# Weight conversion and attention in one scheduling region: earlier stores of finished weight blocks and a first operand cast in three pieces

## The chip, the cores and the metric

The kernel runs on one core of one Trainium2 chip. The metric is the device time of one execution in microseconds (us), from the median of several runs. The core's engines are named as the profile names them: PE (TensorE, matrix products; PEld is its weight load), DVE (VectorE), ACT (ScalarE), POOL (GpSimd) and SP (SyncE), whose queue issues nearly all transfers of this kernel. Each engine works through its own list of instructions in the order in which the list stands.

## The reference

Sigmoid attention for 8 batches of 12 heads (448 positions, 64 wide), whose output, 3584 rows of 768, goes through a gated feed-forward layer.

```python
scores = scale * np.matmul(q, k.transpose(0, 1, 3, 2)) - np.log(S)
attn = 1.0 / (1.0 + np.exp(-scores))
x = np.matmul(attn, v)            # then (batch, position) x (head, width)
gate = 1.0 / (1.0 + np.exp(-(x @ w_gate)))
return (gate * (x @ w_val)) @ w_out
```

The three weights are 64-bit floats: `w_gate` and `w_val` 768 x 1536, `w_out` 1536 x 768.

## The kernel before

**Attention.** A loop of 168 beats (24 times four heads, 7 beats each). In each beat PE forms scores for one tile (line 220), ACT takes their sigmoid (line 223), and PE multiplies the sigmoid of two beats earlier with the values (line 239), into PSUM tiles that exist once each. When such a tile is complete, twice in seven beats, ACT copies one half of it to SBUF (line 263) and DVE adds the other half (`finish_adds`, line 309). Only then may PE begin the next product in that tile, which is four beats later.

**Weights.** `Units.steps` (lines 118 to 159) turns the 64-bit weights into 32-bit floats and forms seven blocks for each unit of work: three of them (`a11`, `a12`, `a22`) are quarters of the tile `wf`, which DVE fills, and four are sums and differences in `wsum`, which POOL fills. There are two `wf` buffers, two `wsum` buffers and three buffers `wr` for the raw weights, which SP loads (line 115). A unit is a generator of steps: for each of its two halves three DVE instructions (lines 124 to 126), then line 128, then line 130; POOL's four sums belong to the last step. The first four units are used in place (13 steps each); the blocks of the other fourteen go to DRAM by seven transfers (line 158). These are put into a list of delayed work, `after(4, store)`, when the generator is called again after the unit's last step, so in the first step of the next unit; they are issued four calls of `tick` later. A tick is one beat in attention, one group of nine products in the feed-forward part.

Steps 1 to 64 are called in the attention loop, one in about 2.4 beats (steps 53 to 58 are the fifth unit, 59 to 64 the sixth). The other 73 are called in the feed-forward loop. A table `turns` gives each operand of that loop a share, and after every group of products steps are called until their part of the 73 has caught up with the part of the shares that is done. In the kernel before, the first operand of all has the share 6 in each of its four groups; of 576 shares in all, its 24 stand for steps 65 to 68.

**Feed-forward.** 300 groups of nine products (line 401) for the gate and value weights, with 25 operands in each of three passes and four groups for each operand; then 50 operands for the output weight. An operand is loaded (`load_x`, line 174, two buffers `src`), its high part is cast by ACT (`high_x`, line 177) into the tile `op` and its low part is formed by DVE (`low_x`, line 180). Both are made for the first operand near the end of the attention loop: the load at the 160th beat, the cast of all 1536 columns at the 164th, the low part at the 165th.

**Order.** Attention stands in one `tc.manual_schedule()` block, the feed-forward part in a second. The program gives the order in which the instructions are written; the scheduler makes each engine's list from it.

Of the kernel before, what the change touches and what calls it, by code (L numbers as in the profile page):

```python
# [14 lines left out]
PSUM = bass.MemoryType.PSUM  # L15
# [24 lines left out]
def sigmoid_attention_glu_kernel(ctx: ExitStack, tc: tile.TileContext, qk, v, wg, wv, wo, out):  # L40
    nc = tc.nc
# [34 lines left out]
    def after(n, fn, store=True):  # L76
        later.append((clock[0] + n, fn, store))

    def tick(flush=False):
        clock[0] += 1  # L80
        due = [e for e in later if e[0] <= clock[0] or flush and e[2]]
        later[:] = [e for e in later if e not in due]
        for _, fn, _ in due:
            fn()
# [6 lines left out]
    def op_tile():  # L91
        return keep.tile([P, 2, 3, F], F32R, tag="op", name="op", bufs=3)
# [4 lines left out]
    def block(tag, n, shape, dtype):  # L97
        return keep.tile(shape, dtype, tag=tag, name=tag, bufs=n)

    class Units:  # L100
# [17 lines left out]
        def steps(self):  # L118
            for s, q, w, j in self.todo:
                f = block("wf", 2, [P, 2, DM], U32)  # L120
                for r in range(2):
                    raw = self.loaded.pop(0)
                    a = f[:, r]
                    nc.vector.tensor_scalar(out=a, in0=raw[:, :, 1], scalar1=0x7FFFFFFF, scalar2=None, op0=ALU.bitwise_and)  # L124
                    nc.vector.tensor_scalar(out=a.bitcast(F32), in0=a.bitcast(F32), scalar1=F64_ZERO, scalar2=None, op0=ALU.max)  # L125
                    nc.vector.tensor_scalar(out=a, in0=a, scalar1=3, scalar2=0x3FFFFFF8, op0=ALU.logical_shift_left, op1=ALU.bitwise_and)
                    yield
                    nc.vector.scalar_tensor_tensor(out=a, in0=raw[:, :, 1], scalar=0xC0000000, in1=a, op0=ALU.bitwise_and, op1=ALU.bitwise_or)  # L128
                    yield
                    nc.vector.scalar_tensor_tensor(out=a, in0=raw[:, :, 0], scalar=29, in1=a, op0=ALU.logical_shift_right, op1=ALU.bitwise_or)  # L130
                    after(2, self.load)
                    if r == 0:
                        yield
                ff = f.bitcast(F32)
                if s < NPASS:
                    a11, a12, a21, a22 = ff[:, 0, :HW], ff[:, 0, HW:], ff[:, 1, :HW], ff[:, 1, HW:]
                else:
                    a11, a21, a12, a22 = ff[:, 0, :HW], ff[:, 0, HW:], ff[:, 1, :HW], ff[:, 1, HW:]
                ss = block("wsum", 2, [P, 4, HW], F32)
                s1, s2, s3, s4 = (ss[:, n] for n in range(4))  # L140
                sub = lambda o, a, b: nc.gpsimd.tensor_tensor(out=o, in0=a, in1=b, op=ALU.subtract)
                nc.gpsimd.tensor_tensor(out=s1, in0=a21, in1=a22, op=ALU.add)  # L142
                sub(s2, s1, a11)
                sub(s3, a11, a21)
                sub(s4, a12, s2)
                blocks = [a11, a12, s2, s3, a22, s1, s4]
                yield
                if s == 0:
                    for i in range(NP):
                        nc.gpsimd.tensor_copy(W[i][:, q, 0], blocks[i])  # L150
                        nc.vector.tensor_tensor(out=W[i][:, q, 1], in0=blocks[i], in1=W[i][:, q, 0].bitcast(F32), op=ALU.subtract)
                        yield
                else:
                    to = [w_src[s][i][:, q] if s < NPASS else o_src[i][:, q] for i in range(NP)]

                    def store(to=to, blocks=blocks):
                        for t, b in zip(to, blocks):
                            nc.sync.dma_start(out=t, in_=b)  # L158
                    after(4, store)

    units = Units()
    weights = units.steps()
# [5 lines left out]
    x_loaded, ops = {}, {}  # L168
# [7 lines left out]
    def high(op, src):  # L176
        nc.scalar.copy(op[:, 0], src)  # L177
# [4 lines left out]
    def high_x(n):  # L182
        if n < len(x_order):
            ops[n] = op_tile()
            high(ops[n], x_loaded[n])
# [4 lines left out]
            load_x(n + 2)  # L190

    halves = (slice(0, HP), slice(HP, P))
    with tc.manual_schedule(), tc.tile_pool(name="att", bufs=2) as att, tc.tile_pool(name="sc", bufs=2, space=PSUM) as scp, \
            tc.tile_pool(name="av", bufs=1, space=PSUM) as avp:
        loads, avs, pending, adds = {}, {}, [], []

        def load_qk(m):
            if m < B * NQ:
                loads[m] = [att.tile([P, 2, 2 * S], F32, tag="qk", name="qk")]
                if m > 0:  # L200
                    nc.sync.dma_start(out=loads[m][0], in_=qk[m // NQ, m % NQ])
# [10 lines left out]
        def scores(m, g):  # L212
            qkt = loads[m][0]

            sc = second_pair() if (m, g) == (0, LAG) else scp.tile([P, 2, 512], F32, tag="sc", name="sc")
            for h in range(2):
                for u in range(2):
                    p = u if g == 3 else g // 4
                    k0 = S + (3 * P if g == 3 else g % 4 * P + u * HP)
                    nc.tensor.matmul(sc[halves[u], h, :S], lhsT=qkt[halves[h], p, k0:k0 + HP], rhs=qkt[halves[h], p, :S],  # L220
                                     start=True, stop=True)
            a = att.tile([P, 2, S], F32, tag="a", name="a", bufs=3)
            nc.scalar.activation(a, sc[:, :, :S], AF.Sigmoid, bias=bias, scale=scale)  # L223
            return a

        def values(m, g, a):
            vt = loads[m][1]
            for u in range(2):
                p = u if g == 3 else g // 4
                key = (2 * m + p, u)  # L230
                start = g == (3 + (u == 0) if p else 0)
                if start and p == 0:
                    avs[key] = avp.tile([P, 512], F32, tag=f"av0{u}", name="av")
                elif start and u == 1:
                    pair = second_pair()
                    avs.update({(2 * m + p, w): pair[:, w] for w in range(2)})
                last = (3 if u == 0 else 2) if p == 0 else 6
                for h in range(2):
                    nc.tensor.matmul(avs[key][halves[h], :S], lhsT=vt[halves[u], g, h], rhs=a[halves[u], h],  # L239
                                     start=start, stop=g == last)  # L240
            if g == 3:
                finish(2 * m)
            if g == 6:
                finish(2 * m + 1)
# [21 lines left out]
        def sub(o, a, b):  # L266
            nc.gpsimd.tensor_tensor(out=o, in0=a, in1=b, op=ALU.subtract)
# [79 lines left out]
        sc = scp.tile([P, 2, 512], F32, tag="sc", name="sc")  # L347
# [5 lines left out]
        beats, beat, done = B * NQ * 7, 0, 0  # L353
        for m in range(B * NQ):
            for g in range(7):
                pending.append((m, g, scores(m, g)))
                if len(pending) > LAG:
                    values(*pending.pop(0))
                if g == 0:
                    load_qk(m + 1)  # L360
                if g == LAG:
                    load_v(m + 1)
                if m == 0 and g <= LAG:
                    units.load()
                tick()
                beat += 1
                while done < N_FIRST and done * (beats - 12) < beat * N_FIRST:
                    next(weights)
                    done += 1
                finish_adds()  # L370
                if beat > 24 and sum(map(len, later_parts)):
                    next(w for w in later_parts if w).pop(0)()
                if beat == beats - 8:
                    load_x(0)
                    load_x(1)
                if beat == beats - 4:
                    high_x(0)
                if beat == beats - 3:
                    low_x(0)
        while pending:  # L380
# [4 lines left out]
        low_x(1)  # L385
        tick(flush=True)

    with tc.manual_schedule(), tc.tile_pool(name="mm", bufs=8, space=PSUM, reuse_waits="tile") as mm:

        def bank():  # L390
            return mm.tile([P, F], F32, tag="mm", name="acc")
# [56 lines left out]
        with tc.tile_pool(name="ff", bufs=1, reuse_waits="tile") as ff:  # L448
# [3 lines left out]
            def store_h(p, i, j, h):  # L452
# [4 lines left out]

            turns = {(s, p, r): (6, 5, 3, 3, 1, 1, 1)[r] if SETS[p] is PAIR else (6, 5)[r % 2]
                     for s in range(NPASS) for p in range(NSET - (1 if s < NPASS - 1 else 2)) for r in range(len(SETS[p]))
                     if s == 0 or p > 0 or r > 1}  # L460
            done, groups, all_groups = 0, 0, sum(turns.values()) * NQUAD
            for s in range(NPASS):
                for p in range(NSET):
# [4 lines left out]
                    for r, (i, _) in enumerate(SETS[p]):  # L468
                        for q in range(NQUAD):
                            d, t, jl = st[q], q % 2, q // 2  # L470
# [30 lines left out]
                            elif i in (2, 3):  # L501
                                k = "u2" if i == 2 else "u3"
                                d[k] = unit(k, 4)
                                add(d[k], acc, d["s1"])
                            else:
                                k, to = {4: ("s1", 1), 5: ("u3", 6), 6: ("u2", None)}[i]
# [160 lines left out]
```

## Time and profile before

| | |
|---|---|
| median of 3 runs | 1190.94 us (1190.78 to 1191.88) |
| profiled execution | 1191.03 us, of which the span from its first to its last instruction is 1189.2 us |
| PE busy | 1178.9 us, 99% of the span |
| DVE, ACT, POOL busy | 59%, 41%, 25% of the span |
| DMA engines | 65.3% busy for SP's queue |
| mean clock granted to PE | 0.997 of full speed |

A matrix product's row in the trace is longer than the distance to the next one, since products are pipelined and their ends are modelled. Where PE's pace matters, the number of products in a stretch of time says more than the busy share. Idle time in square brackets stands before an instruction, with what ended it.

### The profile page before, as it was taken

The numbers are of one execution on the slowest core, as the hardware profiler recorded it, in microseconds if no ns is written. First come the engines' busy times: TensorE is split into PE (matmuls) and PEld (weight loads), VectorE is DVE, ScalarE is ACT, GpSimd is POOL, SyncE is SP. The second block draws the span as 40 slices with busy tenths as digits, with TensorE's granted clock in tenths as the row PEclk, the third lists the DMA queues.
The fourth block names the chain that finished last, engine by engine and source line by source line (L and its number), as shares of the span: only waits on it lengthen the run. The fifth ranks groups of instructions, "written<-read, shape, count | busy, mean of one in ns | idle before, by whom it ended". The sixth has DMA issues, their size and how long they took to land.

```text
span 1189.2 us, 17012 instructions
## 1 busy us (share of the span) xinstructions
PE 1178.9 (99%) x6754; PEld 860.8 (72%) x6754; DVE 698.3 (59%) x725; ACT 488.6 (41%) x514; POOL 297.5 (25%) x232
## 2 busy tenths in 40 slices
PE   9999999899999999999999999999999999999998
PEld 3333333348888888888888888888888888888887
DVE  3334334436798848889875888747676542244343
ACT  6777777663323234432232532323445212422320
POOL 1335225143182332344322344404020000000000
PEclk9999999989999999999999999999999999999999
DMA  8588867776588675758857666755876553445431
GB/s 302 166 244 287 268 231 240 259 266 227 208 311 289 237 272 198 245 189 291 313 195 283 227 227 220 256 184 191 292 246 249 177 203 133 156 153 186 170 115 71
DMA packets 105376, 266.95 MB, mean 224 GB/s; under 512 B 19920, under 2 KB 54736, under 8 KB 105296
## 3 DMA queue, kind: packets, MB, share of 16 engines
q1 hardware_dynamic: 105152, 265.73, 65.3%
q8 instruction: 53, 0.87, 0.3%
q14 instruction: 27, 0.22, 0.1%
q10 hardware_dynamic: 144, 0.13, 0.0%
HBM read 178.91 MB, written 86.90 MB: 224 GB/s over the span
## 4 chain that ended last, share of the span: by engine, by line
PE 97%; DMA 1%; DVE 1%; SPq 0%; ACT 0%; issue 0%; DVEq 0%; ACTq 0%
PE acc L401 77%; PE sc L220 10%; PE av L239 10%; DMA wr<-wg 1%; DMA ws<-wf 0%; DMA qk<-qk 0%; SPq L158 0%; DVE wf L130 0%; DVE op L309 0%; DVE wf L124 0%; ACT a L223 0%; DVE wf L128 0%; SPq L270 0%; PE av L220 0%; DVE wf L125 0%
## 5 line engine op out<-in xcount | busy, mean ns | idle before, releaser
L401 PE MATMUL acc<-op,w 128*128 128x512 f32 x3600 | 828.3, 389 | 0.0
L401 PEld LDWEIGHTS acc<-op,w 128*128 128x128 f32 x3600 | 675.8, 188 | 140.8 <-issue 0.7
L180 DVE TENSOR_TENSOR op<-src,op 128x1536 fp32r<-128x1536 f32 x125 | 236.2, 1900 | 106.0 <-ACT op L177 84.3
L177 ACT CAST op<-src 128x1536 fp32r<-128x1536 f32 x125 | 184.6, 1479 | 196.9 <-PE acc L401 162.9
L223 ACT ACTIVATE a<-sc,bias 128x896 f32<-128x896 f32 x167 | 168.1, 1007 | 73.8 <-PE sc L220 69.1
L239 PE MATMUL av<-a,v 64*64 64x448 f32 x1344 | 168.0, 541 | 5.6 <-DVE op L309 5.6
L220 PE MATMUL sc<-qk 64*64 64x448 f32 x1336 | 167.9, 545 | 0.1
L239 PEld LDWEIGHTS av<-a,v 64*64 64x64 f32 x1344 | 53.7, 134 | 83.1 <-issue 74.2
L220 PEld LDWEIGHTS sc<-qk 64*64 64x64 f32 x1336 | 53.0, 135 | 80.2 <-issue 67.7
L408 DVE TENSOR_TENSOR u<-acc,s 128x512 f32<-128x512 f32 x90 | 61.7, 688 | 78.8 <-PE acc L401 78.7
L408 DVE TENSOR_TENSOR u<-acc,u 128x512 f32<-128x512 f32 (+1 forms) x91 | 61.7, 682 | 64.4 <-PE acc L401 63.8
L520 POOL TENSOR_TENSOR t<-u,v 128x512 f32<-128x512 f32 x17 | 26.6, 1566 | 283.6 <-DVE u L411 233.3
L142 POOL TENSOR_TENSOR wsum<-wf 128x384 f32<-128x384 f32 x18 | 19.9, 1106 | 201.2 <-DVE wf L130 201.2
L513 ACT ACTIVATE u<-u 128x512 f32<-128x512 f32 x36 | 22.7, 632 | 97.5 <-DVE u L408 97.5
L408 DVE TENSOR_TENSOR s<-acc,s 128x512 f32<-128x512 f32 x45 | 31.0, 689 | 34.2 <-PE acc L401 34.2
L513 ACT ACTIVATE s<-s 128x512 f32<-128x512 f32 x18 | 11.4, 632 | 96.1 <-DVE s L408 96.1
L401 PE MATMUL acc<-op,wr 128*128 128x512 f32 x198 | 50.2, 389 | 0.0
L309 DVE TENSOR_TENSOR op<-av,op 128x448 f32<-128x448 f32 x24 | 15.0, 623 | 52.6 <-ACT op L263 52.6
L309 DVE TENSOR_TENSOR x<-av,x 128x448 f32<-128x448 f32 x24 | 15.0, 624 | 49.5 <-ACT x L263 49.5
L124 DVE TENSOR_SCALAR wf<-wr 128x768 uint32<-128x768 uint32 x36 | 26.9, 748 | 28.4 <-DMA wr<-wg 17.2
L401 PEld LDWEIGHTS acc<-op,wr 128*128 128x128 f32 x198 | 37.2, 188 | 7.7
L436 DVE TENSOR_TENSOR w<-w 128x1536 fp32r<-128x1536 f32 x21 | 41.1, 1959 | 0.0
(61 smaller groups left out, 723.2 us busy)
## 6 DMA issues: line engine op xcount, KB each, us to landing
src<-xs SPq DMA_DIRECT2D x75, 768.0 KB, 5.1
src<-hs SPq DMA_DIRECT2D x50, 768.0 KB, 5.2
qk<-qk SPq DMA_DIRECT2D x23, 896.0 KB, 5.0
hs<-t SPq DMA_DIRECT2D x78, 256.0 KB, 6.0
w<-ws SPq DMA_DIRECT2D x14, 768.0 KB, 7.1
v<-vv SPq DMA_DIRECT2D x23, 448.0 KB, 4.5
wr<-wg SPq DMA_DIRECT2D x12, 768.0 KB, 6.9
wr<-wv SPq DMA_DIRECT2D x12, 768.0 KB, 6.7
```

Source lines behind the costliest of these rows:

```text
L124: nc.vector.tensor_scalar(out=a, in0=raw[:, :, 1], scalar1=0x7FFFFFFF, scalar2=None, op0=ALU.bitwise_and)
L177: nc.scalar.copy(op[:, 0], src)
L180: nc.vector.tensor_tensor(out=op[:, 1], in0=src, in1=op[:, 0].bitcast(F32), op=ALU.subtract)
L220: nc.tensor.matmul(sc[halves[u], h, :S], lhsT=qkt[halves[h], p, k0:k0 + HP], rhs=qkt[halves[h], p, :S], start=True, stop=True)
L223: nc.scalar.activation(a, sc[:, :, :S], AF.Sigmoid, bias=bias, scale=scale)
L239: nc.tensor.matmul(avs[key][halves[h], :S], lhsT=vt[halves[u], g, h], rhs=a[halves[u], h], start=start, stop=g == last)
L309: nc.vector.tensor_tensor(out=x, in0=other, in1=x, op=ALU.add)
L401: nc.tensor.matmul(acc, lhsT=a, rhs=b, start=first and n == 0 and half != 1, stop=n == len(terms) - 1 and half != 0, skip_group_check=not ...
L408: nc.vector.tensor_tensor(out=o, in0=a, in1=b, op=ALU.add)
L436: nc.vector.tensor_tensor(out=w[:, :, 1], in0=w[:, :, 1].bitcast(F32), in1=w[:, :, 0].bitcast(F32), op=ALU.subtract)
L513: nc.scalar.activation(d[k], d[k], AF.Sigmoid)
L520: nc.gpsimd.tensor_tensor(out=o, in0=a, in1=b, op=ALU.subtract)
```

## The change

There are four edits. The store of a unit's blocks is split: the three blocks in `wf` are issued after one tick, the four in `wsum` still after four. Both parts of the kernel stand in one `manual_schedule` block, which is entered once for the whole function. The first operand's load moves from the 160th to the 159th beat, its `op` tile is taken there too, and its cast is made as three casts of 512 columns in beats 162, 163 and 164. The first operand's four groups have no share in `turns` any more, which leaves 552 shares; step 65 is then called in the first group of the second operand.

```diff
-                    def store(to=to, blocks=blocks):
-                        for t, b in zip(to, blocks):
-                            nc.sync.dma_start(out=t, in_=b)
-                    after(4, store)
+                    def store(which, to=to, blocks=blocks):
+                        for i in which:
+                            nc.sync.dma_start(out=to[i], in_=blocks[i])
+                    after(1, lambda store=store: store((0, 1, 4)))
+                    after(4, lambda store=store: store((2, 3, 5, 6)))
...
-    with tc.manual_schedule(), tc.tile_pool(name="att", bufs=2) as att, tc.tile_pool(name="sc", bufs=2, space=PSUM) as scp, \
+    ctx.enter_context(tc.manual_schedule())
+    with tc.tile_pool(name="att", bufs=2) as att, tc.tile_pool(name="sc", bufs=2, space=PSUM) as scp, \
             tc.tile_pool(name="av", bufs=1, space=PSUM) as avp:
...
-                if beat == beats - 8:
+                if beat == beats - 9:
                     load_x(0)
                     load_x(1)
-                if beat == beats - 4:
-                    high_x(0)
+                    ops[0] = op_tile()
+                if beats - 7 < beat < beats - 3:
+                    k = beat - beats + 6
+                    nc.scalar.copy(ops[0][:, 0, k], x_loaded[0][:, k])
...
-    with tc.manual_schedule(), tc.tile_pool(name="mm", bufs=8, space=PSUM, reuse_waits="tile") as mm:
+    with tc.tile_pool(name="mm", bufs=8, space=PSUM, reuse_waits="tile") as mm:
...
-                     if s == 0 or p > 0 or r > 1}
+                     if (p > 0 or r > 1 if s > 0 else p + r > 0)}
```

## Rows read from the trace of the kernel before

**Rows 1.** Longest piece of the chain of waits: start us, us, what.

```profile
267.35 918.24 PE acc L401 x4050
```

**Rows 2.** Busy time by stretch: length, each engine's busy us, PE clock, DMA.

```profile
20.00:228.20 208.20, 208.20 (x2220) 79.21 (x2214) 79.45 (x115) 156.21 (x179) 75.25 (x90) 1.00 0.75 245
228.20:267.27 39.07, 33.42 (x316) 14.26 (x310) 13.17 (x19) 22.64 (x26) 14.15 (x12) 0.91 0.74 256
245.38:267.27 21.89, 21.89 (x232) 10.23 (x224) 4.62 (x5) 16.95 (x19) 10.85 (x10) 1.00 0.87 302
239.50:245.38 5.88, 5.87 (x32) 2.04 (x36) 3.25 (x5) 1.01 (x1) 3.31 (x3) 0.51 0.35 100
```

**Rows 3.** Timeline of PE, two instructions: start us, us, engine, line [idle before].

```profile
230.00 0.59 PE L239 MATMUL av<-a,v 64*64 64x448 f32 x2 [0.88 <-DVE op L309]
...
239.51 1.01 PE L239 MATMUL av<-a,v 64*64 64x448 f32 x2 [4.76 <-DVE op L309]
```

**Rows 4.** Timeline of DVE from 218 us, and its first weight step after 267 us.

```profile
218.49 0.95 DVE L128 SCALAR_TENSOR_TENSOR wf<-wr,wf 128x768 uint32<-128x768 uint32 x1
225.67 0.56 DVE L124 TENSOR_SCALAR wf<-wr 128x768 uint32<-128x768 uint32 x1 [6.23 <-DMA ws<-wf]
...
229.33 0.62 DVE L309 TENSOR_TENSOR op<-av,op 128x448 f32<-128x448 f32 x1
229.86 0.95 DVE L130 SCALAR_TENSOR_TENSOR wf<-wr,wf 128x768 uint32<-128x768 uint32 x1
...
238.36 0.56 DVE L124 TENSOR_SCALAR wf<-wr 128x768 uint32<-128x768 uint32 x1 [5.88 <-DMA wr<-wg]
...
280.51 0.95 DVE L128 SCALAR_TENSOR_TENSOR wf<-wr,wf 128x768 uint32<-128x768 uint32 x1
```

**Rows 5.** Timeline of SP's queue in the same stretch.

```profile
230.84 0.32 SPq L158 DMA_DIRECT2D ws<-wf  x1
...
232.18 0.42 SPq L115 DMA_DIRECT2D wr<-wg  x1
```

**Rows 6.** Waits of SP's queue: who waited for whom: us, times, longest us.

```profile
SPq L158 <- DVE wf L130: 7.4, 1, 7.4
```

**Rows 7.** Timelines of ACT and PE around the first operand's cast.

```profile
258.59 0.52 ACT L263 COPY x<-av 128x448 f32<-128x448 f32 x1
259.19 1.01 ACT L223 ACTIVATE a<-sc,bias 128x896 f32<-128x896 f32 x1
260.10 1.47 ACT L177 CAST op<-src 128x1536 fp32r<-128x1536 f32 x1
261.46 1.90 ACT L223 ACTIVATE a<-sc,bias 128x896 f32<-128x896 f32 x2
...
261.55 0.54 PE L220 MATMUL sc<-qk 64*64 64x448 f32 x2
...
262.52 1.07 PE L220 MATMUL sc<-qk 64*64 64x448 f32 x8
```

**Rows 8.** ACT's casts by shape: count | busy us, mean ns | idle before.

```profile
L433 ACT CAST w<-w 128x1536 fp32r<-128x1536 f32 x21 | 30.9, 1473 | 0.0
...
L433 ACT CAST wr<-wr 128x768 fp32r<-128x768 f32 x3 | 2.5, 825 | 0.0
```

**Rows 9.** Operand loads, us to landing: whole execution, then those issued from 250.8 us.

```profile
src<-xs SPq DMA_DIRECT2D x75, 768.0 KB, 5.1
...
src<-xs SPq DMA_DIRECT2D x2, 768.0 KB, 8.2
```

**Rows 10.** Early feed-forward part: two stretches, then two DVE instructions.

```profile
275.50:324.50 49.00, 49.00 (x218) 40.59 (x217) 36.55 (x43) 15.31 (x16) 7.17 (x6) 1.00 0.65 223
324.50:349.00 24.50, 24.50 (x109) 20.28 (x108) 24.19 (x20) 5.53 (x5) 20.34 (x11) 1.00 0.83 272
...
269.35 2.60 DVE L180 TENSOR_TENSOR op<-src,op 128x1536 fp32r<-128x1536 f32 x1 [0.76 <-ACT op L177]
...
333.45 1.64 DVE L124 TENSOR_SCALAR wf<-wr 128x768 uint32<-128x768 uint32 x1
```

## The prediction

> **What bounds the kernel now.** I read the chain of waits first. Its last piece is 4050 products of the feed-forward part, one after another for 918.24 us [rows 1]: 226.7 ns each without a gap, so nothing done there for DVE, ACT or the queues can shorten those 918 us. They begin at 267.35 us. What can still move is therefore the attention part before them, and I compared its pace by stretch. From 20 to 228.2 us PE makes 2220 products in 208.2 us, 0.0938 us each, at full clock [rows 2]. From 228.2 us to the end of attention it makes 316 in 39.07 us, where the old pace needs 29.6. Taking off the last stretch (232 products from 245.38 us, in 21.89 us) leaves 84 products in 17.18 us, which should take 7.88: **9.3 us are lost between 228 and 245 us**, and about another 0.1 to 0.5 us after it (0.1 by the count of 232; 0.5 if the four products already running at the edge are taken off).
>
> The timeline of PE shows what the 9.3 us are: idle for 0.88 us before 230.00 and for 4.76 us before 239.51, both ended by DVE's line 309 [rows 3], and after the second a stretch of 5.88 us at about half clock (0.51, the 1.2 GHz level), in which 32 products take what should take 3.0 us, so 2.9 us more [rows 2]. That makes 8.5; the other 0.8 us is the pace around the two gaps (idle time is counted from ends that are modelled, which lie later than the next product could start).
>
> Then DVE: why was line 309 late? As written, after step 60 (line 128 at 218.49) come the add of beat 146 (line 309) and step 61 (line 130). In the trace there comes instead, at 225.67, line 124 of a new unit, after 6.23 us of waiting for a transfer of `wf`, then that unit's further steps, and only at 229.33 the add; step 61 follows at 229.86 [rows 4]. At 238.36 once more a line 124 that waited, 5.88 us for raw weights [rows 4], stands ahead of an add, the one that ends PE's second gap [rows 3]. These jumped instructions are steps 65 to 68, which are written in the second block, in the first operand's groups. The count confirms it: 24 of 576 shares of 73 steps are 3.04, so four steps, and the first weight instruction of DVE in the feed-forward part is a line 128 at 280.51, which is step 69 and not 65 [rows 4]. So instructions of the second block were put between those of the first on DVE's list, and DVE works through its list in order. SP's list shows the same: a store of the sixth unit (written after step 65) stands at 230.84, having waited 7.4 us for line 130 [rows 5, 6], and the raw-weight load at 232.18, on which the 5.88 us hang, stands behind it.
>
> **The change part by part.**
>
> One block. What I read from the lists is that inside a block they follow the written order; steps 65 to 68 are the only DVE work that jumped. With one block, add 146 comes right after step 60, step 61 after it, add 149 after step 62. None of these waits for a store or a load: step 61 has no idle time in front of it [rows 4], and the raw weights of steps 62 to 64 are asked for at the 134th beat (lines 131 and 115: two ticks after step 55). The adds then come as from 20 to 228 us, where PE lost nothing. Gain 9.3 us: the 0.88 and 4.76 us, the 0.8 around them, and the 2.9 us of low clock, which followed the 4.76 us of idling.
>
> The `turns` edit. Steps 65 to 68 now run from the second operand on. Their cost as measured in attention: six instructions of 0.56 and two of 0.95, 5.3 us of DVE [rows 4]. Beside a busy POOL line 124 takes 1.64 us (at 333.45 [rows 10]), 2.9 times as long; all eight stretched like that would be 15.5 us. They are not simply added at one place: by the shares, the first seven operands get steps 65 to 72 instead of 69 to 75, so eight steps in place of seven. DVE is idle there for 12.4 of 49 us [rows 10], so one more step (1.7 to 4.9 us) fits. What is late next is the low part of an operand: the second one's ends at 269.35 + 2.60 = 271.95 us and is first used after 36 products, at 267.35 + 36 x 0.2267 = 275.5, so 3.6 us of slack [rows 1, 10]. I take zero cost; the bound is one step late by 4.9 - 3.6 = 1.3 us, and below zero nothing, since this part has no gap to give back.
>
> The early store. Three of seven issues of each unit move three ticks ahead on SP (4.5 us in attention, 6 in the feed-forward part). They pass the transfers of those ticks, so behind them queue the loads of lines 174, 201 and 115. They wait for line 130 of the last step, which DVE has passed when the next unit's first step comes. SP's one long wait at line 158 was the jumped store [rows 6]. It frees `wf` earlier, which was the 6.23 us wait; with the order mended nobody waits for that, so alone it is worth nothing more. Zero, bounds -0 and +0.5 us (a store that waits, by the 0.3 to 1 us of one issue [rows 5]).
>
> The cast in pieces. One cast of 1536 columns (1.47 us) made ACT late: two sigmoids run back to back from 261.46, and PE's scores come at 262.52 [rows 7], some 0.2 us behind their pace (0.97 us for the eight products from 261.55, where eight usually take 0.75). By the two shapes (1.473 at 1536 columns, 0.825 at 768 [rows 8]) a column costs 0.84 ns and an instruction 0.18 us, so a piece is 0.61 us by my estimate. A beat is 16 products, 1.50 us, a sigmoid 1.01, so each beat has 0.5 us to spare, and one of the three beats also has a copy of 0.52 [rows 7]. 3 x 0.61 + 0.52 - 3 x 0.5 is 0.85 us of backlog, less 0.1 for each of three starts that overlap the end before (as the cast at 260.10 does), so 0.6. Now it is 0.77 (the sigmoid due at 259.19 + 1.50 = 260.69 starts at 261.46) and costs PE 0.2: the 0.2 shrinks to 0.05 or so. Gain 0.15, bounds 0.2 and -0.3. [...]
>
> The earlier load. The first piece is due behind the sigmoid two beats before that at 259.19, so at about 259.19 - 3.0 + 1.0 = 257.2 us [rows 7]; the load was issued at 250.86. Landing took 8.2 us there, with the jumped stores in the way, and 5.1 us in the middle of all loads [rows 9]. By the first it is 1.9 us late, by the second 1.2 us early. I take the second, because the sixth unit's stores (seven times 192 KB) leave this stretch with the steps that caused them.
>
> **Sum.** The profiled execution took 1191.03 us, its span 1189.2, so 1.8 us lie outside. 1191.03 - 9.3 - 0.15 = 1181.6 us. The median of the runs is 0.09 lower; I leave that.
>
> **Rivals.** First, the handover has a new wait: the piece of the cast waits 1.9 us for its load, or the first feed-forward products wait for PSUM or an operand. For it: 8.2 us to landing in that stretch; against: the stores leave. It costs 1.9 us, and 2.9 more if PE falls to the low clock again: 1183.5 to 1186.4.
>
> Second, the change doesn't mend the order, because it was not the border of the blocks that let the steps jump. Against: only steps written behind the border jumped. Then the early store still frees `wf` three beats (4.5 us) sooner: the first gap (1.2 us with its surroundings) goes, the second, which hangs on the raw load, stays: about 1190.
>
> Third, slower: DVE becomes the bound in the feed-forward part. From 324.5 to 349 us it is busy for 24.19 of 24.5 us [rows 10]. If the four moved steps are not absorbed before that, up to 15.5 us of DVE work at POOL-slowed durations come on top of a full engine; it decides at 3.6 us of lateness, from where an operand's low part comes after its first use. 15.5 - 3.6 = 11.9 us of PE waiting give 1193.5, and one fall of the clock 2.9 more, 1196.4. Against: DVE idles 12.4 us before that stretch, and the shares put only one step more there.
>
> **How the numbers follow.** A measurement of this kernel can tell about 0.2%, 2.4 us, from no change. Forecast as above, 1181.0 to 1182.8: 0.83. New wait at the handover: 0.08. Order not mended: 0.05. DVE the bound: 0.04. Of the last, 0.01 is a milder form that ends near 1190 and 0.03 the full price. The order not mended counts as the same but for 0.01 of it. So faster 0.92, same 0.05, slower 0.03. The floor is 1191.03 - 9.3 - 0.5 = 1181.2, less 0.3 for the spread of runs: low end 1180.9. The high end takes in the bounds of the unknown costs (1.3, 0.5 and 0.3 us) and the first rival's near case: 1184.0.
>
> **What would show it.** Right: no `[idle before]` on PE between 228 us and the first feed-forward product, which begins near 258 us; add 146 directly behind step 60 on DVE; no wait of line 124 for `ws<-wf` or `wr` there; the first weight step of the feed-forward part is a line 124; PE's clock at full between 20 us and the end; 918 us for 4050 products again. Wrong: a gap before the sigmoid of beats 162 to 164 with the load as its releaser (first rival), line 124 still ahead of line 309 (second), gaps between feed-forward products that DVE's `op` or an add releases (third).

## The result, and the profile after

| | before | after |
|---|---|---|
| median of six runs | 1191.24 us | 1181.26 us (1180.76 to 1181.47) |
| ratio, with its 95% interval | | 0.9917 [0.9904, 0.9931] |
| profiled execution | 1191.03 us, span 1189.2 | 1181.45 us, span 1179.7 |
| 316 attention products from 228.2 us | 39.07 us | 29.50 us |
| 4050 products of the feed-forward part | 918.24 us | 918.26 us |

The change makes the kernel 0.8% faster. The six runs of before include one of 1715.63 us, which the ratio leaves out; without it their median is 1190.94 us. In the two profiled executions the difference is 9.58 us, and the two stretches of the table account for it: 39.07 - 29.50 = 9.57 us in the end of attention, nothing in the feed-forward part.

The chain of waits of after (start us, us, what; [rows 1] is its counterpart) still has the 4050 products as its last piece. They only begin at 257.77 us instead of 267.35:

```profile
257.77 918.26 PE acc L405 x4050
```

Busy time by stretch (columns as in [rows 2]): up to 228.2 us the same number of products, to within one, in the same time as before; after it the 316 products now take 29.50 us, with the clock at 1.00 where it was 0.91.

```profile
20.00:228.20 208.20, 208.20 (x2221) 138.31 (x2217) 80.75 (x117) 156.44 (x179) 75.51 (x90) 1.00 0.77 249
228.20:257.70 29.50, 29.50 (x316) 18.86 (x308) 8.11 (x9) 22.90 (x28) 14.17 (x12) 1.00 0.68 243
```

The waits of PE (who waited for whom: us, times, longest us) are these two in the whole execution. Both lie outside the stretch, and neither is for an add: line 66 sets a constant at the start. The gaps of 0.88 and 4.76 us of [rows 3] have no successor.

```profile
PE sc L353 <- DVE bias L66: 1.0, 1, 1.0
PE sc L222 <- DMA qk<-qk: 0.3, 1, 0.3
```

DVE's timeline shows the cause (start us, us, engine, line; line 311 is the add that was 309; to be held against [rows 4]). Behind step 60 (line 128 at 218.55) stands the add of beat 146, at 224.02 and not at 229.33, then step 61 (line 130), then line 124 of step 62, which waits for nothing. The first weight step of the feed-forward part is a line 124 at 269.88, step 65, where it was a line 128, step 69:

```profile
218.55 0.95 DVE L128 SCALAR_TENSOR_TENSOR wf<-wr,wf 128x768 uint32<-128x768 uint32 x1
224.02 0.62 DVE L311 TENSOR_TENSOR op<-av,op 128x448 f32<-128x448 f32 x1 [4.52 <-ACT op L265]
224.56 0.95 DVE L130 SCALAR_TENSOR_TENSOR wf<-wr,wf 128x768 uint32<-128x768 uint32 x1
225.43 0.55 DVE L124 TENSOR_SCALAR wf<-wr 128x768 uint32<-128x768 uint32 x1
...
228.53 0.62 DVE L311 TENSOR_TENSOR op<-av,op 128x448 f32<-128x448 f32 x1 [1.36 <-ACT op L265]
...
269.88 0.55 DVE L124 TENSOR_SCALAR wf<-wr 128x768 uint32<-128x768 uint32 x1
```

In ACT's timeline (line 381 is a piece of the cast, 225 the sigmoid, 265 the copy) sigmoids are due every 1.50 us: the second one below is on time, the third is due at 249.61 and comes 0.34 us late, the fourth 0.25 us late. The last line here is the view of the tile `src` from 240 to 262 us: three loads landed after 4.5, 5.4 and 5.9 us.

```profile
246.61 1.01 ACT L225 ACTIVATE a<-sc,bias 128x896 f32<-128x896 f32 x1 [0.49 <-PE sc L222]
247.52 0.61 ACT L381 CAST op<-src 128x512 fp32r<-128x512 f32 x1
248.11 1.01 ACT L225 ACTIVATE a<-sc,bias 128x896 f32<-128x896 f32 x1
249.02 0.52 ACT L265 COPY x<-av 128x448 f32<-128x448 f32 x1
249.43 0.63 ACT L381 CAST op<-src 128x512 fp32r<-128x512 f32 x1
249.95 1.02 ACT L225 ACTIVATE a<-sc,bias 128x896 f32<-128x896 f32 x1
250.85 0.62 ACT L381 CAST op<-src 128x512 fp32r<-128x512 f32 x1
251.36 1.03 ACT L225 ACTIVATE a<-sc,bias 128x896 f32<-128x896 f32 x1
...
DMA to landing us min/median/max: 4.5/5.4/5.9
```

### The profile page after: what moved, and what is told of

It is laid out like the page before. It is cut to its first block, busy times and chain, and to the rows that moved or that the text cites. A ratio compares the mean times of both kernels' runs of the same rounds, so it can differ in the third digit from the quotient of the medians.

```text
span 1179.7 us, 17017 instructions
## 1 busy us (share of the span) xinstructions
PE 1174.8 (100%) x6754; PEld 927.5 (79%) x6754; DVE 699.2 (59%) x725; ACT 488.9 (41%) x516; POOL 302.0 (26%) x232
## 4 chain that ended last, share of the span: by engine, by line
PE 99%; DMA 0%; DVE 0%; DVEq 0%; issue 0%
PE acc L405 78%; PE sc L222 11%; PE av L241 11%; DMA qk<-qk 0%; PE av L222 0%; DVE u L412 0%; DVEq L665 0%
## 5 line engine op out<-in xcount | busy, mean ns | idle before, releaser
L181 DVE TENSOR_TENSOR op<-src,op 128x1536 fp32r<-128x1536 f32 x125 | 233.8, 1881 | 107.3 <-ACT op L178 70.3
L222 PE MATMUL sc<-qk 64*64 64x448 f32 x1336 | 234.2, 539 | 0.3 <-DMA qk<-qk 0.3
L241 PE MATMUL av<-a,v 64*64 64x448 f32 x1344 | 234.1, 536 | 0.0
L241 PEld LDWEIGHTS av<-a,v 64*64 64x64 f32 x1344 | 88.2, 133 | 43.6 <-issue 0.9
L222 PEld LDWEIGHTS sc<-qk 64*64 64x64 f32 x1336 | 87.7, 134 | 43.5 <-DMA qk<-qk 1.3
L524 POOL TENSOR_TENSOR t<-u,v 128x512 f32<-128x512 f32 x17 | 32.4, 1906 | 279.8 <-DVE u L415 190.2
L142 POOL TENSOR_TENSOR wsum<-wf 128x384 f32<-128x384 f32 x18 | 23.3, 1292 | 209.4 <-DVE wf L130 209.4
L130 DVE SCALAR_TENSOR_TENSOR wf<-wr,wf 128x768 uint32<-128x768 uint32 x36 | 41.9, 1165 | 0.7
```

Of the source, the lines that this page charges most:

```text
L181: nc.vector.tensor_tensor(out=op[:, 1], in0=src, in1=op[:, 0].bitcast(F32), op=ALU.subtract)
```

## The experiments

Two groups of kernels: each of the four edits alone in the kernel before, then four that set the suspected cause by hand. The theory: PE lost its time because adds came late on DVE behind steps 65 to 68, and the one block puts the adds back. Its rivals: another of the edits brings the gain (the store that frees `wf`, the cast in pieces, the later share of steps), or the border of the blocks does something else than let steps jump. The kernel before was run beside each group: 1191.08 us in the median beside the first four kernels, 1190.86 beside the others. The last column is the start of the 4050 products in the chain of waits, 267.35 us in before and 257.77 in after.

| kernel | median us | ratio to before, 95% interval | first feed-forward product, us |
|---|---|---|---|
| one block alone | 1181.44 | 0.9920 [0.9905, 0.9935] | 257.81 |
| `turns` alone | 1181.27 | 0.9918 [0.9902, 0.9935] | 257.67 |
| early store alone | 1189.83 | 0.9991 [0.9981, 1.0000] | 265.97 |
| cast in pieces alone | 1191.78 | 1.0007 [0.9998, 1.0017] | 268.40 |
| after, jump written by hand | 1190.67 | 0.9995 [0.9986, 1.0004] | 266.21 |
| after, four steps earlier | 1180.92 | 0.9920 [0.9904, 0.9937] | 257.06 |
| before, three steps jump | 1183.41 | 0.9939 [0.9925, 0.9954] | 259.14 |
| after, steps still later | 1181.54 | 0.9923 [0.9908, 0.9938] | 258.17 |

### One block alone

The kernel before with a single `manual_schedule` block; stores, cast and `turns` as they were.

```diff
-    with tc.manual_schedule(), tc.tile_pool(name="att", bufs=2) as att, ...
+    ctx.enter_context(tc.manual_schedule())
+    with tc.tile_pool(name="att", bufs=2) as att, ...
...
-    with tc.manual_schedule(), tc.tile_pool(name="mm", bufs=8, ...
+    with tc.tile_pool(name="mm", bufs=8, ...
```

> The kernel before with one scheduling block and nothing else of the change. Theory (order of DVE's list): steps 65 to 68 no longer stand ahead of the adds, so both gaps of PE and the low clock go: 9.3 us less than before, 1181.6 to 1182.2 us, first feed-forward product near 258.0 us, a delay of 0.2 us left at the whole cast. Rival (the stores or the cast carry the gain): 1188 us or more.

Measured 1181.44 us (1181.28 to 1181.65): the whole gain, and 0.2 us below the expected range. The stretch from 228.2 us has the same 316 products in the same 29.50 us as after. The second line and those behind it are ACT's timeline around the uncut cast: the sigmoid due at 249.68 + 1.50 = 251.18 starts at 251.95, 0.77 us late, just as late as in [rows 7].

```profile
228.20:257.70 29.50, 29.50 (x316) 10.99 (x308) 7.59 (x9) 22.77 (x26) 14.08 (x12) 1.00 0.67 239
...
249.68 1.01 ACT L224 ACTIVATE a<-sc,bias 128x896 f32<-128x896 f32 x1
250.59 1.46 ACT L177 CAST op<-src 128x1536 fp32r<-128x1536 f32 x1
251.95 1.91 ACT L224 ACTIVATE a<-sc,bias 128x896 f32<-128x896 f32 x2
```

So the late sigmoid costs PE nothing here: 316 products in 29.50 us with it and without it. The cast in pieces, the earlier load and the early store are not needed for any of the gain.

### The `turns` edit alone

Two blocks as before; only the first operand's groups lose their share, so that no weight step stands in them.

```diff
-                     if s == 0 or p > 0 or r > 1}
+                     (p > 0 or r > 1 if s > 0 else p + r > 0)}
```

> The kernel before, two blocks, and only the first operand's share taken out of the table. Theory: what matters is that no weight step stands ahead of the adds; the steps now are written behind the second operand's low part, which itself waits, so they don't jump although there are two blocks: also 1181.6 to 1182.2 us. Rival (the border of the blocks as such costs time): the gaps stay, 1189 to 1191 us.

Measured 1181.27 us (1181.21 to 1181.34), the whole gain again, with the border still there, and 0.3 us below the expected range. On DVE (line 309 is the add here) the add follows step 60 directly, as in after:

```profile
228.20:257.60 29.40, 29.40 (x315) 20.26 (x307) 7.59 (x9) 22.63 (x26) 14.18 (x12) 1.00 0.68 238
...
218.45 0.95 DVE L128 SCALAR_TENSOR_TENSOR wf<-wr,wf 128x768 uint32<-128x768 uint32 x1
223.92 0.62 DVE L309 TENSOR_TENSOR op<-av,op 128x448 f32<-128x448 f32 x1 [4.52 <-ACT op L263]
```

Steps written in the first operand's groups jump the border; written behind the second operand's first group they don't. Either edit therefore mends the order by itself, and the two gains are one gain, not a sum.

### The early store alone

```diff
-                    after(4, store)
+                    after(1, lambda store=store: store((0, 1, 4)))
+                    after(4, lambda store=store: store((2, 3, 5, 6)))
```

> The kernel before and only the early store of the three wf blocks. Theory: the steps still jump, but wf is free some 3 us sooner; the first gap goes, the second (which waits for raw weights behind a store on SP's queue) gets shorter by 1 to 3 us; 1185 to 1190 us, two low-clock outcomes: 2.9 us with it, 0 without. Rival (the wait for the transfer of wf is the whole cause): 1181.6 to 1182.2 us.

Measured 1189.83 us. This kernel still has the wrong order, with the store of `wf` three ticks earlier. The rows, in this order: SP's issue of that store; DVE's step 60 and the two line 124 that jumped (6.23 and 5.88 us of waiting in [rows 4]); PE's second gap and the low-clock stretch behind it; and what the queue did from 216 to 226 us (packets, MB, share of 16 engines; then issues, KB each, us to landing).

```profile
218.03 1.44 SPq L158 DMA_DIRECT2D ws<-wf  x3
...
218.97 0.95 DVE L128 SCALAR_TENSOR_TENSOR wf<-wr,wf 128x768 uint32<-128x768 uint32 x1
225.04 0.56 DVE L124 TENSOR_SCALAR wf<-wr 128x768 uint32<-128x768 uint32 x1 [5.12 <-DMA ws<-wsum]
...
238.17 0.56 DVE L124 TENSOR_SCALAR wf<-wr 128x768 uint32<-128x768 uint32 x1 [6.34 <-DMA wr<-wg]
...
239.32 1.01 PE L240 MATMUL av<-a,v 64*64 64x448 f32 x2 [5.21 <-DVE op L310]
...
239.30:242.60 3.30, 3.28 (x20) 1.28 (x24) 3.26 (x5) 0.00 (x0) 0.79 (x1) 0.50 0.19 70
...
q1 hardware_dynamic: 1611, 3.63, 100.1%
...
ws<-wf SPq DMA_DIRECT2D x3, 192.0 KB, 5.8
```

The first gap is gone from PE's waits; the second is 5.21 us where it was 4.76. The stretch at about half clock behind it is shorter: 20 products in 3.30 us lose 1.4 us, where before it was 2.9. Counted from step 60 (line 128), the last of the three transfers of `wf` is issued 3 us earlier than before (at 219.0, step 60 at 218.97; before, 221.57 and 218.49), but line 124 starts only 1.1 us earlier (6.07 us behind step 60 in place of 7.18). The DMA engines have no idle share left there (in before they were 96.5% busy in the same stretch), and a transfer of `wf` takes 5.8 us to landing, so the last lands near 224.8; the transfer of `wsum` that the row names as the releaser lands about then too, and the rows don't part the two. In the medians the early store is worth 1.25 us while the order is wrong (0 to 2.3 by the interval), and, by the kernel with one block alone, nothing where it is right.

### The cast in three pieces alone

```diff
-                if beat == beats - 8:
+                if beat == beats - 9:
...
-                if beat == beats - 4:
-                    high_x(0)
+                    ops[0] = op_tile()
+                if beats - 7 < beat < beats - 3:
+                    k = beat - beats + 6
+                    nc.scalar.copy(ops[0][:, 0, k], x_loaded[0][:, k])
```

> The kernel before and only the earlier load and the cast in three pieces. Theory: both gaps stay; 0.15 us less than before, so within 0.3 us of it. Rival (a late first piece, since the load landed after 8.2 us in this stretch of the kernel before): ACT waits up to 2 us for the load and PE with it, up to 2 us more than before.

Measured 1191.78 us, 0.7 us more than before in the median, where 0.15 less was expected; the interval of the ratio, 0.9998 to 1.0017, doesn't part it from no change. With the stores of the jumped steps still in the stretch, the load takes 8.1 us, and the first piece of the cast (line 379) waits for it on ACT:

```profile
258.73 0.62 ACT L379 CAST op<-src 128x512 fp32r<-128x512 f32 x1 [1.20 <-DMA src<-xs]
...
src<-xs SPq DMA_DIRECT2D x2, 768.0 KB, 8.1
```

That is the first rival of the prediction, in small: its wait is real wherever those stores remain, and in after they don't.

### After, with the jump written by hand

One block, all four edits, but steps 61 to 67 are called at beat 144 and step 68 at beat 146, all ahead of the add of beat 146; the rest of the table is shortened by four.

```diff
-    N_REST = (NPASS * NQUAD + HJ - NQUAD - 2) * 6 + 1
+    N_REST = (NPASS * NQUAD + HJ - NQUAD - 2) * 6 + 1 - 4
...
-                while done < N_FIRST and done * (beats - 12) < beat * N_FIRST:
+                while done < N_FIRST + 4 and (60 <= done < 67 or done >= 60 and beat >= 146 or done < 60 and done * (beats - 12) < beat * N_FIRST):
```

> The changed kernel (one block), with steps 61 to 68 written by hand ahead of the add of beat 146 (61 to 67 at beat 144, 68 at beat 146) and the 69 others paced as before. Theory (an add behind a step that waits for raw weights): step 68 waits for its raw weights, which are loaded after step 61, so add 146 comes at 233 to 237 us instead of 224; PE stops once for 5 to 8 us and runs 1.7 to 2.9 us longer at the low clock: 1188 to 1192 us. Rival (the border of the two blocks costs time of itself): 1181.3 us, as there is one block.

Measured 1190.67 us, the time of the kernel before, with a single block and with everything else that the change does. DVE's timeline, PE's gap and the stretch behind it:

```profile
219.81 0.96 DVE L130 SCALAR_TENSOR_TENSOR wf<-wr,wf 128x768 uint32<-128x768 uint32 x1
...
224.74 1.18 DVE L124 TENSOR_SCALAR wf<-wr 128x768 uint32<-128x768 uint32 x1 [0.32 <-DMA ws<-wf]
...
228.51 1.64 DVE L128 SCALAR_TENSOR_TENSOR wf<-wr,wf 128x768 uint32<-128x768 uint32 x1
...
232.04 0.56 DVE L124 TENSOR_SCALAR wf<-wr 128x768 uint32<-128x768 uint32 x1 [0.90 <-DMA wr<-wg]
233.71 1.15 DVE L311 TENSOR_TENSOR op<-av,op 128x448 f32<-128x448 f32 x2
...
234.38 1.01 PE L241 MATMUL av<-a,v 64*64 64x448 f32 x2 [4.92 <-DVE op L311]
...
234.38:240.00 5.62, 5.62 (x36) 2.04 (x40) 0.48 (x1) 1.01 (x1) 0.00 (x0) 0.58 1.00 311
```

The time and the place of the add are as expected, the way there is not: I had reckoned with a long wait for raw weights, and it is 0.90 us, with 0.32 us for the store. The add comes at 233.71 because the fourteen instructions of eight steps stand before it from 219.81 us on: 9.8 us at their usual lengths. They wait for 1.2 us in all, and four of them take about twice that (1.18 us for 0.56, 1.64 for 0.95) while POOL forms its sums, from 224.5 us. So it is the lateness of the add that costs, by whatever it comes about.

### After, with four steps earlier but not in an add's way

```diff
-                while done < N_FIRST and done * (beats - 12) < beat * N_FIRST:
+                while done < N_FIRST and (done >= 60 or done * (beats - 12) < beat * N_FIRST):
```

> The changed kernel with steps 61 to 64 written together at beat 144, ahead of the adds of beats 146, 149 and 153. None of these steps waits for a transfer. Theory (it is the wait that costs, not the place): DVE is through them at 224.0 us, when add 146 is due, so 1181.3 us, within 0.3. Rival (any weight step ahead of the adds makes them late): a gap of PE of 1 us or more, 1182.5 to 1186 us.

Measured 1180.92 us, 0.1 us below the expected range and not told apart from after. Steps 61 to 64 now stand ahead of add 146, as the jumped ones did, but they wait for nothing and are done in time: the add starts at 223.36. The last line here is from PE's timeline in before, the products ahead of its first gap.

```profile
222.49 0.96 DVE L130 SCALAR_TENSOR_TENSOR wf<-wr,wf 128x768 uint32<-128x768 uint32 x1
223.36 0.62 DVE L311 TENSOR_TENSOR op<-av,op 128x448 f32<-128x448 f32 x1
...
228.20:256.98 28.78, 28.78 (x308) 10.74 (x300) 6.05 (x7) 22.25 (x27) 9.62 (x8) 1.00 0.69 233
...
228.20 0.92 PE L239 MATMUL av<-a,v 64*64 64x448 f32 x4
```

Work ahead of the add is harmless as long as the add is not late. How late it may be can be estimated from before. The four products from 228.20 us put the next one at 228.20 + 4 x 0.0938 = 228.58. It came at 230.00, so 1.4 us behind its pace and 0.67 us after the add's start (229.33). An add at about 227.9 would by this have cost nothing, and in after it comes at 224.02: about 4 us to spare.

### Before, with three steps that jump instead of four

```diff
+            turns[0, 0, 0] = 4
             done, groups, all_groups = 0, 0, sum(turns.values()) * NQUAD
```

> The kernel before, two blocks, with share 4 instead of 6 for the first operand: three steps (65 to 67) stand in its groups and jump, step 68, which waits for raw weights, doesn't. Theory: the first gap stays (1.2 us with its surroundings), the second and the low clock go: 1182.5 to 1183.2 us. Rival (both gaps come from the transfers of wf): 1189 to 1191 us.

Measured 1183.41 us. DVE's two adds here are line 309; the second one no longer has a step waiting for raw weights ahead of it.

```profile
225.01 0.58 DVE L124 TENSOR_SCALAR wf<-wr 128x768 uint32<-128x768 uint32 x1 [6.23 <-DMA ws<-wf]
...
227.26 1.21 PE L239 MATMUL av<-a,v 64*64 64x448 f32 x4
...
229.36 0.59 PE L239 MATMUL av<-a,v 64*64 64x448 f32 x2 [0.89 <-DVE op L309]
231.75 0.62 DVE L309 TENSOR_TENSOR op<-av,op 128x448 f32<-128x448 f32 x1
...
228.20:259.07 30.87, 29.98 (x309) 12.46 (x309) 10.89 (x15) 22.16 (x25) 14.15 (x12) 1.00 0.82 299
```

This kernel splits the loss: the first gap alone costs 1183.41 - 1181.26 = 2.1 us against after, the second gap and the low clock behind it 1190.86 - 1183.41 = 7.5 us. I had expected 1182.5 to 1183.2, with 1.2 us for the first gap; in the stretch it is 30.87 - 309 x 0.0938 = 1.9 us. Most of that is the gap itself: by the four products from 227.26 us the next was due at 227.64, and it came at 229.36, 1.7 us late. The row marks only 0.89 us of idling, because it counts from the modelled end of those four (227.26 + 1.21 = 228.47). Behind the gap PE's two streams of products run out of step until they join again: in its timeline eight products from 235.05 us take 1.01 us instead of 0.75.

### After, with the steps still later

No share for the first seven operands at all, to test whether DVE becomes the bound in the feed-forward part.

```diff
-                     (p > 0 or r > 1 if s > 0 else p + r > 0)}
+                     (p > 0 or r > 1 if s > 0 else p > 0)}
```

> The changed kernel with no share for the first seven operands: all 73 steps run from the eighth operand on, where DVE was busy for 24.19 of 24.5 us, 11 % denser than now. Theory (3.6 us of slack in the operands' low parts): one step more in that set, up to 4.9 us of DVE, PE loses 0 to 1.3 us: 1181.3 to 1182.6 us. Rival (DVE is the bound there): operands late in several groups and the low clock, 1184 to 1190 us.

Measured 1181.54 us. Two stretches of the feed-forward part, first of after, then of this kernel, and the chain of waits of the latter:

```profile
266.00:315.00 49.00, 49.00 (x218) 40.57 (x217) 37.44 (x47) 15.32 (x16) 7.76 (x6) 1.00 0.73 251
315.00:340.00 25.00, 25.00 (x112) 20.71 (x111) 24.65 (x19) 5.54 (x5) 18.82 (x11) 1.00 0.88 289
```

```profile
266.00:315.00 49.00, 49.00 (x218) 40.62 (x217) 28.50 (x33) 15.40 (x16) 1.82 (x2) 1.00 0.51 165
315.00:340.00 25.00, 25.00 (x112) 20.73 (x111) 24.59 (x21) 5.54 (x5) 19.46 (x11) 1.00 0.77 253
...
258.17 918.24 PE acc L405 x4050
```

DVE is busy for 24.59 of 25 us, as it is in after, and PE makes its 112 products all the same; the 4050 take 918.24 us. Moving even more steps behind the first operands costs nothing that can be seen.

## Why the prediction was right, point by point

**What bounds the kernel.** As said: the 918 us are unchanged, and all that moved lay between 228 and 257 us. The 9.3 us came out as 9.57. The rest are the 0.1 to 0.5 us after 245 us, which the prediction saw but left out of the sum: PE's pace recovers there too, with the cast uncut as well (one block alone), so it belonged to what the gaps leave behind.

**One block.** The step holds: the written order inside a block is DVE's order, and the block alone gives the whole gain (1181.44). What was incomplete is the share of the edits. I put the `turns` edit at zero beside the block; it is zero there, but alone it gives the same gain (1181.27), since it takes the steps away that jumped. Two ways to mend one fault: neither adds to the other.

**The gaps.** The first was priced at 1.2 us with its surroundings and costs 2.1, by the kernel with three steps that jump. Its row's 0.88 us counts from a modelled end; by the products around it PE stood 1.4 us behind its pace. So this 1.2, and with it the second rival's price, was too small, while the 0.8 us that the sum adds for both gaps together covers the difference. The second, with the low clock behind it, costs 7.5 us, where [rows 2, 3] gave 4.76 + 2.9 = 7.7. The granted clock behaved as [rows 2] had it: about half behind the long gaps (0.51 before, 0.50 with the early store, 0.58 with the jump by hand, each behind 4.8 to 5.2 us of idling), 1.00 behind the short one of 0.89 us. The Trainium skill ("TensorE: Matmul & The Clock Gate", HAM oscillation — how this bites in real kernels) says that waits between bursts of products can bring back the half clock; these rows agree for the long gaps.

**The cast in pieces.** This is the term that was mis-sized: 0.15 us forecast, nothing measured. The pieces take 0.61 to 0.63 us, as the estimate from [rows 8] had it, and the backlog is 0.34 us where I said 0.6. But the 0.2 us of PE that I read from [rows 7] were not the uncut cast's doing alone: with the uncut cast and a sigmoid just as late, PE loses nothing (one block alone). They fit the out-of-step pace that PE has behind a gap: with three steps that jump, eight products at 235.05 us are 0.26 us slow in the same way, long before the cast. That this was their cause is argued, not shown. The Trainium skill ("ScalarE: Activation LUTs", What ACT_TABLE_LOAD costs) gives an ACTIVATE with immediate scale and bias 186 ns plus 0.833 ns per element. Taken for a cast of 512 columns that is 0.61 us, by estimate, and this trace agrees.

**The earlier load.** I took 5.1 us to landing; the first operand's load landed after 4.5 and the next after 5.9 us. No piece waited. The first piece came 0.5 us after the landing (242.50 + 4.5 = 247.0 against 247.52), so the margin was 0.5 us and not 1.2: the load was issued 5.0 us ahead of that piece, where I had 257.2 - 250.86 = 6.3. Nor did the edit bring the load forward. With one block alone, where it stands a beat later in the program, SP issues it at 242.54 us, and in both kernels right behind the same store (at 242.13 and 242.16).

**The early store.** Zero, as said. SP's wait of 7.4 us at line 158 for line 130 [rows 6] is gone.

**The rivals.** The first (a wait at the handover) appears only where the jumped stores stay: 1.2 us on ACT with the cast in pieces alone. The second had about 1190 us for an early store with the order unmended; that kernel takes 1189.83. That the time fits is in part luck: the rival counted only the first gap as gone, at 1.2 us, and had `wf` free 4.5 us sooner. The last store of `wf` was issued 3 us sooner and line 124 came 1.1 us sooner, and in the profiled execution a shorter stretch at the low clock gave part of the gain. The third (DVE the bound) has its premise, 24.65 of 25 us busy, but not its effect; the moved steps are absorbed in the idle time before, as reckoned.

**What stays open.** Why the scheduler places steps of a later block ahead of earlier work, and why it leaves those behind the second operand's first group where they are, no run shows. A fourth buffer for raw weights, which might have taken the second wait away without touching the order, wasn't tried.

## What to carry to other kernels

Compare the order in which an engine's instructions stand in the trace with the order in which they are written: an instruction that stands too early and waits there holds up all that is behind it, and the engine that suffers is another one. Price such a find by how late the work behind it comes, beyond its slack, and add the low clock that a long gap leaves; don't price it by the wait itself. Where a change holds several edits that all touch one fault, try each alone before crediting one of them.

## What the runs showed of the hardware that I had not expected

An earlier issue can buy less than its own lead: with the last store of `wf` 3 us ahead, the step behind it came 1.1 us earlier. The time to landing of these transfers grew from 4.6 us in the kernel before to 5.8, with the engines 96.5% and 100.1% busy from 216 to 226 us. That the fuller engines are the reason is argued, not shown.

A short gap of PE costs more than the idling marked at it, although the clock stays at 1.00: 1.9 us in the stretch where 0.89 us is marked. By the starts of the products around it the gap is 1.7 us, so most of the difference is that the mark counts from a modelled end.

The start of an execution varies. From 4 to 8 us PE makes 36 products in the profiled execution of after, but 28 in that of the kernel with the steps still later (busy time by stretch, in this order), and all later times move with it, by up to about 1.1 us between the executions profiled here. So single profiles are compared here from 228 us on, by products in a stretch rather than by where they end.

```profile
4.00:8.00 4.00, 4.00 (x36) 1.31 (x32) 0.00 (x0) 2.45 (x3) 0.00 (x0) 1.00 0.91 279
```

```profile
4.00:8.00 4.00, 4.00 (x28) 1.27 (x24) 0.00 (x0) 2.07 (x3) 0.00 (x0) 1.00 0.96 318
```
